# Other order of the first loads, counts in a shared PSUM bank, and an earlier weight fetch in a routing-attention and mixture-of-experts kernel

## The chip, the cores and the metric

The kernel runs on one core of one Trainium2 chip. The metric is the device time of one execution in microseconds (us); lower is better. TensorE (PE in the profile; PEld is its weight load) multiplies matrices, VectorE (DVE) and ScalarE (ACT) work elementwise, GpSimd (POOL) makes constants and here issues the indirect transfers, SyncE (SP) issues most of the other transfers. Each engine runs its own list of instructions in order and waits on semaphores for the others.

## The reference

Two stages. Attention, in which a query sees only the keys that fall into its own cluster, feeds a mixture of experts, in which each token goes to one expert.

```python
batch, n_heads, seq, head_dim = (4, 8, 768, 64);  n_clusters = 16
q_assign = argmax(einsum('bhsd,hcd->bhsc', q_n, c_n))        # q_n, k_n, c_n: rows over their norms
k_assign = argmax(einsum('bhsd,hcd->bhsc', k_n, c_n))
mask = q_assign[:, :, :, None] == k_assign[:, :, None, :]
scores = where(mask, q @ k^T / sqrt(64), -1e9)
x = softmax(scores) @ v                                      # then to [3072 tokens, 512]

N, D, E, F = (3072, 512, 8, 1024)
logits = x @ w_gate                                          # [3072, 8]
expert_idx = argmax(logits);  gate_w = softmax(logits)[expert_idx]
for e in range(E):                                           # tokens sorted by expert
    y[tokens of e] = relu(x[tokens of e] @ w1[e]) @ w2[e]
out = gate_w * y                                             # in the tokens' own order
```

Everything is float32. How many tokens an expert gets is known only on the chip.

## The kernel before

**Order.** Both parts are written under a manual schedule: the order of the program text is the order of each engine's list. The pools of tiles decide when a buffer may be written again. Of PSUM, pool `ps_s` holds three double banks `sps` for scores, and pool `ps_m` two banks `mps`, which attention outputs, sums, cluster scores and counts take in turn.

**Attention.** The 32 heads are taken as 16 pairs; pair `n` belongs to batch `n // 4`. A pair has 12 units, two halves of the queries by six blocks of keys. A unit is `score` (float32 products of `qT` and `kT` and, on top in the same bank, bfloat16 products of the cluster masks `mq` and `mk`, all at L370; then the exponential on ScalarE, L383, into `A`) and `add_up` (VectorE adds `A` into `acc`, L389). The products with `v` come after the units (`attend`, L395). Next to the units, `at_pair(n, u, f)` hangs other steps on unit `u` of pair `n`:

- `prepare(n + 1, step)` gets the next pair ready: its cluster scores (`similar`, L304), VectorE's choice of the nearest cluster (`assign0` to `assign2`, whose last result is `ohT`, L340), and the copies of it into `mk` on VectorE (L352) and `mq` on ScalarE (L350). Before it, `turn` (L272) transposes `q_in` and `k_in` to `qT` and `kT` on VectorE, two pairs ahead, between the halves of `attend`.
- `sum_up(n - 1)` at unit 2 makes the softmax sums and the gate's part on TensorE, in columns 0 to 191 of an `mps` bank; `weights_of(n - 1)` reads them on VectorE.
- Routing of a batch, in the pairs after it: `gate`, `gate_exp`, `gate_sum`, `choose`, then `count` (two 128 x 8 matmuls, L526 and L527, into an `mps` bank of their own) and `number` (VectorE, L532 to L539, which makes the places `pos_i`; `run` at L533 is the running count; then six indirect transfers from POOL, L541, into the list of tokens `tokens_of`). For batch 2 all of this is packed into pairs 12 and 13, since the first expert turns need it: `rank_first` (L576) picks their experts, `first_turns` (L782) reads their numbers into registers, fetches their token lists (`places`, from `tokens_of` into `sf`) and the weights of turn 0.

**Start.** `load(n)` issues the inputs of a pair. For pair 0, `q` and `k` go as one half on SP's queue and one half on ScalarE's, then `v_in` on SP's queue. `load(1)` follows at once. Then come the constants, TensorE's transposes of the pair 0 inputs and of the normed centroids `cn` (L262), `first_turn` (their copies out of PSUM), `cT` on VectorE, two ScalarE-queue stores of `cT` to memory (`c_normed`, L289), and nine small VectorE copies (L293 to L298) of constants that POOL has made. `prepare(0, ...)` runs through all its steps, and `routing_constants` (POOL) follows.

**Expert turns.** Ten turns `s`, each for one expert and a fixed number of its tokens: 288 and 288 for the two that start on the first three batches alone, then 256, 288, 288, 384, 416, 416, 448, 128. `layer1` (L881 on) forms the first product from seven half-size products per half of the features, in banks `bank` and `sbank`; it calls a hook after each, units 0 to 13 of `h1`. It wants four sums of the weights' quarters, `A[0]` to `A[3]` (`w1_sums`, L743, 1.23 us each on VectorE, `A[1]` from `A[2]`, `A[3]` from `A[1]`), and VectorE adds (L860) between its products. `layer2` (L985 on) does the same for full pairs of row tiles with `V[0]` to `V[3]` (`w2_sums`), with the hooks of `h2`; its results `z` go out through POOL's indirect transfers (L977). The hooks prepare the next turns: `places`, `indices`, `gather` (POOL's indirect loads of rows), `weigh` (VectorE, `xw`), `take` and `turn_rows` (the rows transposed, `xT`), `x_sums`, `first_weights` and `second_weights` (2 MB each, from SP's queue, into one of two sets of buffers, `wa` and `wb`, by turns), and the weights' sums at the units listed in `when`.

In turn 1, `weigh(2)` is at unit 6 of layer 1, `take(2)` and `first_weights(2)` at unit 7, `second_weights(2)` at unit 8, and the sums for turn 2 at units 2 to 6 of layer 2. In turn 0, `places(2)` is at unit 3 of layer 2.

Of the kernel before, what the change touches and what calls it, by code (L numbers as in the profile page):

```python
# [8 lines left out]
F32 = mybir.dt.float32  # L9
# [24 lines left out]
def kernel(  # L34
# [11 lines left out]
    nc = tc.nc  # L46
    B, H, S, D = q.shape
    C = centroids.shape[1]
    P = 128
# [63 lines left out]
    def iota(name, shape, pattern, base, mult):  # L113
        ti = consts.tile(shape, I32, name=name + "_i")
        tf = consts.tile(shape, F32, name=name)
        nc.gpsimd.iota(ti, pattern=pattern, base=base, channel_multiplier=mult)
        nc.gpsimd.tensor_copy(tf, ti)
        return tf
# [44 lines left out]
    with tc.manual_schedule(), ExitStack() as actx:  # L163
# [12 lines left out]
        def load(n):  # L176
            b, hp = divmod(n, HP)
            for d, src, name in ((QIN, q, "q_in"), (KIN, k, "k_in")):
                t = d[n] = ld.tile([P, NI, Q4], F32, name=name)
                if n == 0:  # L180
                    t = d[n] = t.rearrange("p i d -> p (i d)").rearrange("p (j a d) -> p j a d", a=2, d=D)
                    for a in range(2):
                        (nc.sync, nc.scalar)[a].dma_start(out=t[:, :, a, :], in_=src[0, a].rearrange("(p j) d -> p j d", j=NQ))
                    continue
                for r in range(4):
                    s = src[b, 2 * hp + r // 2, :, Q4 * (r % 2) : Q4 * (r % 2 + 1)]
                    nc.sync.dma_start(
                        out=t[Q4 * r : Q4 * (r + 1)].rearrange("t (j a) d -> t j a d", a=4),
                        in_=s.rearrange("(a t j) d -> t j a d", a=4, j=NQ),
                    )  # L190
            VIN[n] = ldv.tile([P, 2, NQ, D], F32, name="v_in")
            for a in range(2):
                nc.sync.dma_start(
                    out=VIN[n][:, a], in_=v[b, 2 * hp + a].rearrange("(p j) d -> p j d", j=NQ)
                )

        cin = consts.tile([P, D], F32)
        nc.scalar.dma_start(out=cin, in_=centroids.rearrange("h c d -> (h c) d"))
        for n in range(2):
            load(n)  # L200

        csq = consts.tile([P, D], F32)
        cs2 = consts.tile([P, 1], F32)
# [5 lines left out]
        nc.scalar.activation(warm, cnrm, AF.Exp, scale=0.0)  # L209
        MQ = [msk.tile([P, S], BF16, name=f"mq{i}") for i in range(2)]  # L210
        MK = [msk.tile([P, S], BF16, name=f"mk{i}") for i in range(2)]
        for i in range(2):
            for t in (MQ[i], MK[i]):
                (nc.gpsimd if i else nc.vector).memset(t, 0.0)

        cT = consts.tile([P, HP, 2, C], F32)
        nc.vector.memset(cT, 0.0)
# [2 lines left out]
        for a in range(2):  # L220
# [2 lines left out]
                in_=moe_w_gate.rearrange("(h a d) e -> a d h e", a=2, d=D)[a],  # L223
            )
        make_identity(nc, ident)
        first_c = iota("first_c", [P, C], [[-1, C]], C, 0)
        ones_s = consts.tile([P, 2, Q4], F32)
        nc.gpsimd.memset(ones_s, 0.0)
# [55 lines left out]
        cv = cps[:, 0:P].rearrange("p (h a c) -> p h a c", a=2, c=C)  # L284
        for a in range(2):
            nc.vector.tensor_copy(cT[D * a : D * (a + 1), :, a, :], cv[D * a : D * (a + 1), :, a, :])
        first_turn(1)
        for a in range(2):
            nc.scalar.dma_start(  # L289
                out=cn_d.rearrange("(h a) d c -> a d h c", a=2)[a], in_=cT[D * a : D * (a + 1), :, a, :]  # L290
            )
        first_cb = consts.tile([P, C], BF16)
        nc.vector.tensor_copy(first_cb, first_c)  # L293
        ksc2 = consts.tile([P, 2], F32)
        kscn2 = consts.tile([P, 2], F32)
        for r in range(4):
            nc.vector.tensor_copy(ksc2[Q4 * r : Q4 * (r + 1)], ksc)
            nc.vector.tensor_copy(kscn2[Q4 * r : Q4 * (r + 1)], kscn)  # L298

        def similar(n):  # L300
            ps = ps_m.tile([P, 512], F32, name="mps")
# [40 lines left out]
        def place(n, w):  # L342
            t, m = OH[n], (MQ, MK)[w][n % 2]
            for h in range(2):
                for a in range(2):
                    g = 2 * w + h
                    dst = m[D * a : D * a + Q4, HS * h : HS * (h + 1)]
                    src = t[Q4 * g : Q4 * (g + 1), :]
                    if w == 0:
                        nc.scalar.copy(dst, src)  # L350
                    else:
                        nc.vector.tensor_scalar(  # L352
                            dst, src, scalar1=ksc2[Q4 * g : Q4 * (g + 1), a : a + 1],
                            scalar2=kscn2[Q4 * g : Q4 * (g + 1), a : a + 1], op0=ALU.mult, op1=ALU.add,
                        )
            if w == 0:
                OH.pop(n)
# [44 lines left out]
                nc.scalar.copy(OT[n][:, h * HS : (h + 1) * HS], O.pop((n, h))[:, 0:HS])  # L402


        def sum_up(n):

            ps = SL[n] = ps_m.tile([P, 512], F32, name="mps")
            for w in range(3):
                for qd in range(4):
                    if w < 2:  # L410
                        c0 = TC * Q4 * (qd % 2)
                        lhsT, rhs = ones_s[:, w, :], ACC[n, qd // 2][:, w, c0 : c0 + TC * Q4]
                    else:
                        lhsT, rhs = wgt[:, n % HP, :], OT[n][:, TC * Q4 * qd : TC * Q4 * (qd + 1)]
                    nc.tensor.matmul(  # L415
                        ps[Q4 * qd : Q4 * (qd + 1), 0 : TC * Q4], lhsT=lhsT, rhs=rhs, start=(w == 0), stop=(w == 2),
                    )
# [103 lines left out]
            nc.vector.tensor_copy(last, pr[:, :, TC - 1])  # L521

        def count(b):
            last = LAST.pop(b)
            cps = CPS[b] = ps_m.tile([P, 512], F32, name="mps")
            nc.tensor.matmul(cps[:, 0:E], lhsT=lt_strict, rhs=last, start=True, stop=True)  # L526
            nc.tensor.matmul(cps[:, E : 2 * E], lhsT=ones_sq, rhs=last, start=True, stop=True)  # L527

# [232 lines left out]
        for n in range(NPAIR):  # L761
            if n:
                at_pair(n, 2, sum_up, n - 1)
                at_pair(n, 2, weights_of, n - 1)
                at_pair(n, 4, rows, n - 1)
                at_pair(n, 4, store, n - 1)
            for u, step in ((2 if n else 4, 1), (5, 2), (7, 3), (8, 4), (11, 5)):
                at_pair(n, u, prepare, n + 1, step)
        for b in range(B - 1):
            n = HP * (b + 1)  # L770
            last = b == B - 2
            at_pair(n, 5 if last else 10, gate, b)
            at_pair(n, 8 if last else 11, gate_exp, b)
            at_pair(n + (not last), 10 if last else 3, gate_sum, b)
            at_pair(n + (not last), 8 if last else 9, choose, b)
            at_pair(n + 2 - last, 0 if last else 4, count, b)
            at_pair(n + 2 - last, 1 if last else 6, number, b)
        n = HP * (B - 1)
        slots = range(len(EARLY))
        at_pair(n + 1, 3, rank_first)  # L780

        def first_turns():  # L782
            for s in slots:
# [44 lines left out]
    with tc.manual_schedule(), ExitStack() as ectx:  # L828
# [269 lines left out]
        for s in range(NS):  # L1098
# [5 lines left out]
            if s == 0:  # L1104
                at(h1, 2, sum_up, n - 1)
                at(h1, 2, weights_of, n - 1)
                at(h1, 3, gate, B - 1)
                at(h1, 3, gate_exp, B - 1)
                at(h1, 5, gate_sum, B - 1)
                at(h1, 5, choose, B - 1)  # L1110
                at(h1, 8, count, B - 1)
                at(h1, 9, number, B - 1)
                at(h1, 11, rows, n - 1)
                at(h1, 11, store, n - 1)
                at(h1, 12, rank_all)
                at(h2, 0, rank_rest)
                at(h2, 3, places, 2)
                at(h2, 7, indices, 2)
                at(h2, 7, gather, 2)
            if s == 3:  # L1120
# [2 lines left out]
            if s < last:  # L1123
                if 2 < s + 2 <= last:
                    places(s + 2)
                if s == 0:
                    first_weights(1)
                elif s > 1:
                    take(s + 1)
                if s == 1:  # L1130
                    at(h1, 6, weigh, 2)
                    at(h1, 7, take, 2)

                    at(h1, 7, first_weights, 2)
                    at(h1, 8, second_weights, 2)
                else:
                    second_weights(s + 1)
                if 0 < s <= last - 2:
                    at(h2, 0, first_weights, s + 2)

                if s == 0:
                    when = ((h2, 1), (h2, 2), (h2, 4), (h2, 5), (h2, 7), (h2, 7))
                elif s == 1:
                    when = ((h2, 2), (h2, 3), (h2, 4), (h2, 5), (h2, 6), (h2, 6))
                else:
                    when = ((h1, 9), (h1, 10), (h2, 1), (h2, 2), (h2, 2), (h2, 5))
                if GR[s + 1]["T"] >= 2 * P:
                    for (h, i), f, a in zip(when, (w1_sums,) * 4 + (w2_sums,) * 2, (2, 1, 0, 3, 2, 0)):
                        at(h, i, f, s + 1, (a,), nc.vector)
                at(h2, 1 if s == 1 else 3, turn_rows, s + 1)  # L1150
                if GR[s + 1]["T"] >= 2 * P:
                    at(h2, 1 if s == 1 else 4, x_sums, s + 1)
# [287 lines left out]
```

## Time and profile before

| what | value |
|---|---|
| runs | 682.28, 679.32, 677.63 us; median 679.32 us |
| the profiled execution | 680.02 us, of which the span of the trace is 678.2 us |
| mean granted TensorE clock | 0.989 of full |
| instructions in the trace | 11364 |
| read from and written to HBM | 74.10 MB and 20.70 MB |
| SP's queue q1 | 43.8% of the 16 DMA engines' time |
| attention pair, usual length by the start of its units | 19.74 us |
| same, pairs 6 and 10 (a batch's routing in them) | 21.02 us |
| same, pair 13 (batch 2's routing, packed) | 22.95 us |

The profile comes from one execution. Busy time is a share of the span. A wait is the idle time of an engine ahead of an instruction, put down to what released it. Rows of the timeline begin with the start of the first instruction and the length of the stretch, both in us, and name line, engine, operation and tiles (out<-in); a bracket gives the idle time ahead of it and its releaser. The slices of the page cut the span into 40 parts of 17.0 us; a digit is a share in tenths.

The three places that the change touches lie at the first 40 us (start), around 276 to 303 us (pairs 13 and 14), and at 363 to 405 us (the end of turn 0 and turn 1).

### The profile page before, as it was taken

What the parts mean: (1) busy time and instruction counts of PE and PEld (TensorE: products, weight loads), DVE (VectorE), ACT (ScalarE), POOL (GpSimd) and SP (SyncE); (2) the same over time, 40 slices, a digit from 0 to 9 for tenths busy, and PEclk for the clock granted to TensorE, in tenths of its full rate; (3) what the DMA queues carried; (4) which work ended last, traced back from release to release, by engine and by line L of the source; (5) the groups of instructions that cost most, each with busy time, mean ns of one, the idle gap of its engine ahead of it and who ended that gap; (6) DMA issues with size and microseconds to landing.
All of it is one profiled execution on the core that took longest, in us unless ns stands there. A gap on an engine that the chain in (4) does not pass through costs nothing.

```text
span 678.2 us, 11364 instructions
## 1 busy us (share of the span) xinstructions
PE 648.1 (96%) x4210; PEld 424.3 (63%) x4210; DVE 512.5 (76%) x909; ACT 301.0 (44%) x524; POOL 124.4 (18%) x145
## 2 busy tenths in 40 slices
PE   4999999999999999999999989999999999999993
PEld 2445444455444454444484879978797977869771
DVE  5889999999999999999887788886868375562300
ACT  2756556667556566556432323333231332413210
POOL 4000000012000300222113522324241422040010
PEclk9899999999999999999999989999999999999997
DMA  9723455433455434356473498667494837523010
GB/s 185 144 51 73 88 94 94 67 70 69 80 94 94 73 73 78 63 152 197 113 264 96 147 388 281 227 261 251 196 288 175 271 127 218 201 73 135 7 49 17
DMA packets 191807, 95.37 MB, mean 141 GB/s; under 512 B 155967, under 2 KB 173887, under 8 KB 190464
## 3 DMA queue, kind: packets, MB, share of 16 engines
q1 hardware_dynamic: 184016, 81.12, 43.8%
q0 software_dynamic: 4928, 12.97, 5.8%
q10 hardware_dynamic: 2800, 0.48, 0.4%
q8 instruction: 35, 0.57, 0.4%
q14 instruction: 28, 0.23, 0.1%
HBM read 74.10 MB, written 20.70 MB: 140 GB/s over the span
## 4 chain that ended last, share of the span: by engine, by line
PE 52%; issue 27%; DVE 8%; DMA 5%; POOL 5%; SPq 2%; ACT 1%; POOLq 0%; DVEq 0%; ACTq 0%
PE sps L370 19%; PE mps L395 15%; PE bank L902 4%; PE bank L1003 3%; PE sbank L902 3%; POOL out_dram L977 3%; PE sbank L1003 2%; PE mps L415 2%; PE bank L1022 2%; PE mps L304 2%; DVE acc L389 2%; POOL xg L672 1%; DMA w<-in_moe_w_dram 1%; DVE a L723 1%; DVE xw L689 1%
## 5 line engine op out<-in xcount | busy, mean ns | idle before, releaser
L383 ACT ACTIVATE A<-sps 128x768 f32<-128x768 f32 x192 | 153.1, 811 | 47.3 <-PE sps L370 46.2
L370 PE MATMUL sps<-qT,kT 64*128 64x384 f32 x768 | 160.2, 496 | 1.9 <-ACT A L383 1.9
L389 DVE TENSOR_TENSOR acc<-acc,A 128x768 f32<-128x768 f32 x128 | 121.4, 948 | 9.7 <-ACT A L383 3.3
L395 PE MATMUL mps<-A,v_in 128*64 128x384 f32 x768 | 127.4, 488 | 0.0
L370 PEld LDWEIGHTS sps<-qT,kT 64*128 64x128 f32 x768 | 66.8, 188 | 57.8 <-issue 51.0
L395 PEld LDWEIGHTS mps<-A,v_in 128*64 128x64 f32 x768 | 53.8, 137 | 70.5 <-issue 62.2
L977 POOL DMA_INDIRECT out_dram<-z,si x30 | 47.8, 1594 | 199.9 <-DVE z L860 170.7
L541 POOL DMA_INDIRECT tokens_of<-tg,pos_i x24 | 27.1, 1128 | 291.8 <-DVE pos_i L539 145.8
L370 PE MATMUL sps<-mq,mk 64*128 64x384 bf16 x384 | 63.4, 324 | 2.7 <-ACT mq L350 2.7
L1022 PE MATMUL bank<-w,h 128*128 128x512 f32 (+2 forms) x224 | 64.4, 596 | 0.0
L672 POOL DMA_INDIRECT xg<-x_rows,gi x30 | 41.4, 1382 | 50.7 <-DVE gi L662 19.3
L350 ACT COPY mq<-ohT 32x384 bf16<-32x384 bf16 x64 | 32.6, 510 | 38.7 <-DVE ohT L340 29.5
L902 PE MATMUL sbank<-xc,a 128*128 128x144 f32 (+4 forms) x288 | 48.0, 310 | 1.4 <-ACT h L920 0.7
L902 PE MATMUL bank<-xT,w 128*128 128x144 f32 (+4 forms) x288 | 47.8, 309 | 0.0
L902 PEld LDWEIGHTS bank<-xT,w 128*128 128x128 f32 x288 | 43.9, 191 | 2.6 <-issue 2.2
L1022 PEld LDWEIGHTS bank<-w,h 128*128 128x128 f32 (+2 forms) x224 | 24.6, 151 | 32.5 <-issue 32.3
L902 PEld LDWEIGHTS sbank<-xc,a 128*128 128x128 f32 x288 | 43.3, 190 | 2.1 <-issue 1.2
L860 DVE TENSOR_TENSOR h<-sbank,p 128x288 f32<-128x288 f32 (+4 forms) x18 | 9.2, 513 | 46.8 <-PE sbank L902 45.7
L370 PEld LDWEIGHTS <-mk 64*128 64x128 bf16 x384 | 19.5, 94 | 28.2 <-DVE mk L352 3.3
L920 ACT ACTIVATE h<-h 128x288 f32<-128x288 f32 (+4 forms) x36 | 17.6, 488 | 41.4 <-DVE h L860 32.6
L689 DVE TENSOR_TENSOR xw<-xg,sf 128x256 f32<-128x256 f32 (+2 forms) x60 | 32.8, 607 | 2.2 <-DMA xg<-x_rows,gi 1.7
L389 DVE TENSOR_TENSOR acc<-A 128x768 f32<-128x768 f32 x32 | 30.3, 947 | 5.1 <-ACT A L383 5.0
(205 smaller groups left out, 884.5 us busy)
## 6 DMA issues: line engine op xcount, KB each, us to landing
w<-in_moe_w_dram SPq DMA_DIRECT2D x20, 2048.0 KB
v_in<-in_v_dram SPq DMA_DIRECT2D x32, 192.0 KB
x_rows<-x SPq DMA_DIRECT2D x64, 96.0 KB
turn_rows<-xw SPq DMA_DIRECT2D x23, 256.0 KB
q_in<-in_q_dram SPq DMA_DIRECT2D x60, 96.0 KB
k_in<-in_k_dram SPq DMA_DIRECT2D x60, 96.0 KB
xs<-turn_rows SPq DMA_DIRECT2D x16, 144.0 KB
xs<-turn_rows SPq DMA_DIRECT2D x8, 208.0 KB
```

The source lines that it names most:

```text
L350: nc.scalar.copy(dst, src)
L370: nc.tensor.matmul(SP[n, h, j][:, a, 0:HS], lhsT=kt[rows, j * P : (j + 1) * P], rhs=qt[rows, h * HS : (h + 1) * HS], start=first, stop=not ...
L383: nc.scalar.activation(A[n, h, j], ps[:, :, 0:HS], AF.Exp, scale=D**-0.5)
L389: nc.vector.tensor_tensor(ACC[n, h], first, A[n, h, j], op=ALU.add)
L395: nc.tensor.matmul(O[n, h][D * a : D * (a + 1), 0:HS], lhsT=VIN[n][:, a, j, :], rhs=A[n, h, j][:, a, :], start=(j == 0), stop=(j == NQ - 1),)
L541: ins = nc.gpsimd.indirect_dma_start(out=t_d[:, :], out_offset=bass.IndirectOffsetOnAxis(ap=pos_i[:, i : i + 1], axis=0), in_=tg[:, b, i, ...
L672: nc.gpsimd.indirect_dma_start(out=xg[0:m], out_offset=None, in_=x_d[0:rows_in, :], in_offset=bass.IndirectOffsetOnAxis(ap=g["gi"][0:m, j ...
L689: nc.vector.tensor_tensor(xw[0:m, :, :, d2 * a : d2 * (a + 1)], xg[0:m].rearrange("p (r a d b) -> p a r b d", r=HP, a=2, b=DB)[:, a], g["s ...
L902: nc.tensor.matmul(ps[:, f * T2 : (f + 1) * T2], lhsT=w[:, k, (2 * j + f) * P : (2 * j + f + 1) * P], rhs=x[:, k, :], start=first and f + ...
L977: ins = nc.gpsimd.indirect_dma_start(out=out[:, :], out_offset=bass.IndirectOffsetOnAxis(ap=GR[s]["si"][0:rows, j : j + 1], axis=0), in_=z ...
L1003: nc.tensor.matmul(ps[:, 0:H], lhsT=x[:, k, :], rhs=y[:, k, :], start=first and k == 0, stop=k == 3, skip_group_check=not first,)
L1022: nc.tensor.matmul(ps[i * m : (i + 1) * m, :], lhsT=h[:, f, j * P : j * P + m], rhs=w[:, f, :], start=(k == 0), stop=(k == FB // n - 1),)
```

## The change

It has three parts.

**Start.** `load(0)` no longer brings `v_in`; that moves into a function `load_v`. The two stores of `c_normed` go from ScalarE's queue to SP's, directly after `cT`; `load_v(0)` and all of `load(1)` are issued behind them. `MQ[1]` and `MK[1]` are zeroed on POOL after `ident`, not ahead of it. The nine small copies go from VectorE to POOL. Of pair 0's four `mq` copies, the two of the second half go from ScalarE to POOL.

**Counts.** For pairs other than the last, `sum_up` leaves its bank in `BANK`, and `count`, now always at unit 2 and registered after `sum_up` and the next pair's `similar`, writes into columns 256 on of that bank, where it took a bank of its own before. `weights_of` is registered after it. For batch 2, `choose` goes from unit 8 to 10 of pair 12, `gate_sum` from 10 to 9, `count` from unit 0 to 2 of pair 13, `number` from 1 to 3, `rank_first` from 3 to 4. For batches 0 and 1, `count` goes from unit 4 to 2 of pairs 6 and 10; `number` stays at unit 6.

**Turn 2's weights.** `first_weights(2)` goes from unit 7 of turn 1's layer 1 to unit 3 of turn 0's layer 2, behind `places(2)`. In turn 1, the sums `A[2]` and `A[1]` for turn 2 go from units 2 and 3 of layer 2 to units 9 and 10 of layer 1, and `A[0]` and `A[3]` from units 4 and 5 of layer 2 to units 2 and 3.

```diff
@@ load @@
+            if n:
+                load_v(n)
+
+        def load_v(n):
+            b, hp = divmod(n, HP)
             VIN[n] = ldv.tile([P, 2, NQ, D], F32, name="v_in")
@@
-        for n in range(2):
-            load(n)
+        load(0)
@@
-        for i in range(2):
-            for t in (MQ[i], MK[i]):
-                (nc.gpsimd if i else nc.vector).memset(t, 0.0)
+        for t in (MQ[0], MK[0]):
+            nc.vector.memset(t, 0.0)
@@
         make_identity(nc, ident)
+        for t in (MQ[1], MK[1]):
+            nc.gpsimd.memset(t, 0.0)
@@ after cT @@
+        for a in range(2):
+            nc.sync.dma_start(
+                out=cn_d.rearrange("(h a) d c -> a d h c", a=2)[a], in_=cT[D * a : D * (a + 1), :, a, :]
+            )
+
+        load_v(0)
+        load(1)
         first_turn(1)
-        for a in range(2):
-            nc.scalar.dma_start(
-                out=cn_d.rearrange("(h a) d c -> a d h c", a=2)[a], in_=cT[D * a : D * (a + 1), :, a, :]
-            )
         first_cb = consts.tile([P, C], BF16)
-        nc.vector.tensor_copy(first_cb, first_c)
+        nc.gpsimd.tensor_copy(first_cb, first_c)
@@
-            nc.vector.tensor_copy(ksc2[Q4 * r : Q4 * (r + 1)], ksc)
-            nc.vector.tensor_copy(kscn2[Q4 * r : Q4 * (r + 1)], kscn)
+            nc.gpsimd.tensor_copy(ksc2[Q4 * r : Q4 * (r + 1)], ksc)
+            nc.gpsimd.tensor_copy(kscn2[Q4 * r : Q4 * (r + 1)], kscn)
@@ place @@
-                        nc.scalar.copy(dst, src)
+                        (nc.gpsimd.tensor_copy if n == 0 and h else nc.scalar.copy)(dst, src)
@@ sum_up @@
             ps = SL[n] = ps_m.tile([P, 512], F32, name="mps")
+            BANK[:] = [ps] if n < NPAIR - 1 else []
@@ count @@
-            cps = CPS[b] = ps_m.tile([P, 512], F32, name="mps")
+            cps = CPS[b] = BANK.pop()[:, 2 * P : 4 * P] if BANK else ps_m.tile([P, 512], F32, name="mps")
@@ steps of the pairs @@
                 at_pair(n, 2, sum_up, n - 1)
-                at_pair(n, 2, weights_of, n - 1)
@@
-            at_pair(n + (not last), 10 if last else 3, gate_sum, b)
-            at_pair(n + (not last), 8 if last else 9, choose, b)
-            at_pair(n + 2 - last, 0 if last else 4, count, b)
-            at_pair(n + 2 - last, 1 if last else 6, number, b)
+            at_pair(n + (not last), 9 if last else 3, gate_sum, b)
+            at_pair(n + (not last), 10 if last else 9, choose, b)
+            at_pair(n + 2 - last, 2, count, b)
+            at_pair(n + 2 - last, 3 if last else 6, number, b)
+        for n in range(1, NPAIR):
+            at_pair(n, 2, weights_of, n - 1)
@@
-        at_pair(n + 1, 3, rank_first)
+        at_pair(n + 1, 4, rank_first)
@@ turn 0 @@
                 at(h2, 3, places, 2)
+                at(h2, 3, first_weights, 2)
@@ turn 1 @@
                     at(h1, 7, take, 2)
-
-                    at(h1, 7, first_weights, 2)
                     at(h1, 8, second_weights, 2)
@@
-                    when = ((h2, 2), (h2, 3), (h2, 4), (h2, 5), (h2, 6), (h2, 6))
+                    when = ((h1, 9), (h1, 10), (h2, 2), (h2, 3), (h2, 6), (h2, 6))
```

More of the change, by code (lines that the diff above doesn't have):

```diff
@@ L286 @@
             nc.vector.tensor_copy(cT[D * a : D * (a + 1), :, a, :], cv[D * a : D * (a + 1), :, a, :])
-        first_turn(1)
         for a in range(2):
-            nc.scalar.dma_start(
+            nc.sync.dma_start(
                 out=cn_d.rearrange("(h a) d c -> a d h c", a=2)[a], in_=cT[D * a : D * (a + 1), :, a, :]
             )
+        load_v(0)
+        load(1)
+        first_turn(1)
         first_cb = consts.tile([P, C], BF16)
-        nc.vector.tensor_copy(first_cb, first_c)
+        nc.gpsimd.tensor_copy(first_cb, first_c)
         ksc2 = consts.tile([P, 2], F32)
@@ L402, in attend @@
                 nc.scalar.copy(OT[n][:, h * HS : (h + 1) * HS], O.pop((n, h))[:, 0:HS])
+        BANK = []
         def sum_up(n):
             ps = SL[n] = ps_m.tile([P, 512], F32, name="mps")
+            BANK[:] = [ps] if n < NPAIR - 1 else []
             for w in range(3):
```

## The prediction

> **What bounds the kernel now.** I read the page first (shares, slices), then TensorE's waits, then the timelines of TensorE, VectorE and the queues where those waits lie.
>
> ```profile
> PE 648.1 (96%) x4210; PEld 424.3 (63%) x4210; DVE 512.5 (76%) x909; ACT 301.0 (44%) x524; POOL 124.4 (18%) x145
> PEclk9899999999999999999999989999999999999997
> ```
>
> TensorE is busy for 648.1 of 678.2 us: some 30 us of gaps and what a half clock stretches are all that reordering can win. TensorE's waits (us, times, longest) say where they are:
>
> ```profile
> PE sps L262 <- POOL kscn L241: 5.1, 1, 5.1
> PE sps L370 <- ACT mq L350: 2.7, 2, 2.5
> PE sbank L1003 <- DVE z L860: 2.6, 3, 2.0
> PE sps L262 <- DMA k_in<-in_k_dram: 1.6, 1, 1.6
> PE mps L304 <- DVE run L533: 1.5, 1, 1.5
> ```
>
> The change has a part at the last four. The 5.1 us ahead of the first transpose is put down to POOL, but `ident` was written by 3.62; the first `q` halves are what lands at 5.06, and they stay first. The start, from the timeline (start, length):
>
> ```profile
> 8.42 1.51 PE L262 MATMUL sps<-ident,k_in 128*128 128x128 f32 x6 [1.60 <-DMA k_in<-in_k_dram]
> 16.04 2.10 ACT L350 COPY mq<-ohT 32x384 bf16<-32x384 bf16 x4 [5.58 <-DMA tokens_of<-none]
> 18.16 2.21 ACT L383 ACTIVATE A<-sps 128x768 f32<-128x768 f32 x3
> ```
>
> The `k` transposes wait for their load, a VectorE chain follows to `ohT` (16.00), then ScalarE makes four copies before its first exponential. The second place is pair 13 to 14. VectorE's waits from 241 to 331 us are this one row, and its gap ends at 240.74; with it, both engines where pair 15's clusters are scored:
>
> ```profile
> DVE acc L389 <- ACT A L383: 0.8, 1, 0.8
> 301.90 0.93 DVE L272 STREAM_TRANSPOSE kT<-k_in 128x768 f32<-128x768 f32 x1
> 302.82 0.49 PE L304 MATMUL mps<-qT,cT 128*32 128x384 f32 x2
> 302.89 0.52 PE L304 MATMUL mps<-kT,cT 128*32 128x384 f32 x2
> ```
>
> For 90 us VectorE waits for nothing, and at 302.83 it hands over `kT` just as TensorE asks (302.89). There the two engines are level. The third place is turn 1, VectorE's and TensorE's rows:
>
> ```profile
> 383.54 1.23 DVE L723 TENSOR_TENSOR v<-w,v 128x1024 f32<-128x1024 f32 x1
> 384.67 0.46 DVE L860 TENSOR_TENSOR h<-sbank,p 128x288 f32<-128x288 f32 x1
> 385.19 1.25 PE L902 MATMUL sbank<-xT,a 128*128 128x144 f32 x8
> 398.00 1.23 DVE L723 TENSOR_TENSOR a<-w 128x1024 f32<-128x1024 f32 x1 [1.77 <-DMA w<-in_moe_w_dram]
> 399.26 1.23 DVE L723 TENSOR_TENSOR a<-w,a 128x1024 f32<-128x1024 f32 x1
> 400.40 0.42 DVE L860 TENSOR_TENSOR z<-sbank,p 128x256 f32<-128x256 f32 x1
> 400.87 3.66 PE L1003 MATMUL sbank<-w,hs 128*128 128x256 f32 x8 [2.02 <-DVE z L860]
> 404.36 1.05 PE L902 MATMUL bank<-xT,w 128*128 128x128 f32 x8
> ```
>
> Turn 2's weights land at 398, two sums queue ahead of the add that TensorE waits for, and the eight matmuls after the gap take 3.49 us to the next row where the block before took 1.73 (395.23 to 396.96). The stretches' table (PE busy, PEld busy, DVE, ACT, POOL, granted clock) says why:
>
> ```profile
> 397.50:400.80 3.30, 1.35 (x7) 0.84 (x5) 2.77 (x4) 0.00 (x0) 0.00 (x0) 1.00 1.05 408
> 400.90:404.20 3.30, 3.30 (x8) 2.67 (x9) 3.28 (x4) 0.00 (x0) 1.64 (x1) 0.50 1.09 454
> ```
>
> So the place costs 2.02 + 1.76 = 3.78 us.
>
> **Part A, the start.** Before, `v_in(0)` and pair 1's loads are issued from 2.25 on and share the DMA engines with the second half of `k` (ScalarE's queue, issued 1.92). The other half had landed by 6.27, when ScalarE's queue, which waits for it, issues `wgt`. Without the company both should be there by then, and TensorE, busy with `q` and `cn` until 6.82, goes on at 6.85 instead of 8.42: -1.57. `ohT` moves from 16.00 to 14.43. ScalarE then makes two `mq` copies (0.51 each), POOL the other two, needed only half a pair later. The first exponential waits for the second masked matmul, 17.13 - 1.57 = 15.56, plus 0.32 and 0.06: 15.95 instead of 18.16, that is -2.21. The nine small VectorE copies cost nothing before (VectorE then waited 0.58 for TensorE) and nothing on POOL: nine of 0.18 after 5.0 end at 6.7, and `first_cb` is wanted at 12.3.
>
> What is moved must still fit. SP's queue: `c_normed` waits for `cT` (7.35), two issues of 0.69 to 8.8, `v_in(0)` 1.12 to 9.9, `q_in(1)` 2.71 to 12.6, `k_in(1)` 2.88 to 15.5; from the end of four `xs` issues to their use it is 2.8 us (363.86 to 366.61), so `k_in(1)` is there at 18.3. VectorE wants it at 17.0, stalls 1.3 and ends `kT(1)` at 19.3; TensorE asks at about 20. Hidden, narrowly; VectorE has waits of 0.41, 0.83 and 1.73 (23.24, 25.02, 39.64) to catch up. `tokens_of<-none` and pair 2's loads behind them slip 3 us and are wanted after 34. POOL's 4.6 us of routing constants (4.95 to 9.6) move behind its `mq` copies, to 16 to 21, beside VectorE's dense work. The Trainium skill, "GPSIMD Engine Reference", Key points, says that GpSimd shares its SBUF interfaces with VectorE and contends with its two-input operations, and Engine selection gives elementwise work to VectorE. The trace has no such overlap to price; nearest are POOL's one-input copies (0.22 for 24 columns). By the rule VectorE could lose up to those 4.6 us; its 3 us of waits take most, so I book 0, and 1.6 at the bad end. A half clock lies at 18.6 to 21.9 in this execution; it would come again, over a thinner stretch: -0.4 (0 to -0.8). A: -2.6 (-1.0 to -3.5).
>
> **Part B, the counts.** In pairs 6 and 10 the two count matmuls (0.26 each) only move two units earlier: 0. The attention output's first bank now waits for `number`'s read: L533 ends at 228.47 + 0.17 = 228.64, TensorE starts there at 228.89; hidden by 0.25, else a few tenths. In pair 13 the bank's wait (1.50) goes. What is late next: `kT(14)` (281.13, a wait of about 0.5) stays. Pair 13 takes 22.95 us (276.25 to 299.20), pair 6 with the same work 21.02, so TensorE gains 1.93. But VectorE does the same operations in another order and gains nothing: at 302.89 TensorE must again wait for `kT(15)`. Kept: 0.1. `number` now stands behind two adds and `weights_of`, so pos_i comes at 286.0 instead of 283.1; `tokens_of` lands some 3 us later (about 296.4), SP's `sf` issues end at 299 and land by 301, VectorE reads at 302.76: hidden. `rank_first` is 1.8 us later; SP's register loads follow its stores anyway. B: -0.1 (-1.9 to +0.4).
>
> **Part C, turn 2's weights.** The 2 MB go out behind `places(2)`, about 367; the DMA slices there are nearly idle until 378, so at the 5 to 9 us that such a fetch takes (389.04 to 398) they are in before 376. SP's `sf(3)` stands behind them and is wanted at 377.81: hidden. The wait at 398 goes, and w2(2) comes earlier. But the first-layer sums `A[2]` and `A[1]` now stand at layer-1 units 9 and 10 of turn 1, in VectorE's list right behind `v` (383.54) and ahead of the add of 384.67, whose bank the matmuls of 385.19 overwrite. VectorE is late there (its `xw` waits 0.58 and 1.12 for gathers), so 2.40 us (398.00 to 400.40) go straight in: the add ends at 387.53, TensorE stalls 2.4. Layer 2 follows 2.4 later on both; `A[0]` and `A[3]` still stand ahead of the `z` add: 398.63 + 2.40 = 401.03 against a wanted 398.70 + 2.40, a further 0.4. Then the clock. The Trainium skill, "TensorE: Matmul & The Clock Gate", Why this matters, has it fall after a whole window of idling, about 3.4 us, so a gap of 2.4 would be free: cost 2.8, gain 1.0. The row above speaks against it: 2.02 us of gap were enough. By the row 1.7 comes on top, less the 0.4 it hides: cost 4.1, loss 0.3. I take the row three times in four: C about 0 (+1.2 to -3.8, the last if VectorE isn't late).
>
> **Sum.** -2.6 - 0.1 + 0 = -2.7 against the profiled execution's 680.02 (span 678.2, 1.8 around it): 677.3. The median of the runs is 679.32, 0.7 lower, so 676.6.
>
> **The rivals.** (1) VectorE isn't the bound: its rows are close-packed only because TensorE feeds them so. Then B keeps 1.9 and C 2.8: 676.6 - 1.8 - 2.8 = 672.0. For it: up to pair 12 VectorE waits 0.5 to 0.8 for ScalarE in most second pairs (202.41, 240.74). Against: none from 241 to 331. (2) The start doesn't carry: `k_in(1)` or POOL holds VectorE beyond its slack, A is 0 to -0.6: 679.0. (3) Slower: the 2 MB collide. If SP reaches the fetch only after about 373 (its `places` wait for tokens), the gathers of turn 2's rows at 374.87 and 378.10 queue beside 2 MB, `xw` slips by up to 5 us, and with it the add of 384.67: 5 more of stall and no gain in turn 1, 676.6 + 5.5 = 682.1. It decides from 2.8 us of slip on. Against: SP issued those loads at 365.34 unhurried. That the fetch isn't earlier at all is excluded by SP's list.
>
> **How the numbers follow.** My forecast 0.62 (own range 674.6 to 678.6), rival 1 0.17, rival 2 0.13, rival 3 0.08. Leaving out a tenth at each end: 672.0 to 680.0. One per cent, 6.8 us, is about what a measurement of this kernel can tell from no change: faster means below 672.5, which is over half of rival 1 and an edge of mine, 0.13; slower, above 686.1, only rival 3 doubled, 0.02.
>
> **What would show it.** `k` transposes at 6.9 and the first exponential near 16; no wait on `run` in pair 13 and in its place waits for `kT` in pairs 13 and 14; `a` sums before the add in turn 1's layer 1, and TensorE waiting there for over 2 us, with no wait for weights after. It is wrong if TensorE waits less than 1 us there, or if pair 14's end moves by more than the start.

## The result, and the profile after

| | before | changed |
|---|---|---|
| median | 679.55 us (22 runs) | 677.25 us (22 runs) |
| ratio | | 0.9966, 95% interval 0.9953 to 0.9979 |
| profiled execution | 680.02 us, span 678.2 | 678.35 us, span 676.3 |
| mean granted clock in it | 0.989 | 0.989 |

The change takes 2.3 us off (1.4 to 3.2 by the interval), which is clear of noise but less than the one per cent that the prediction calls faster. All lines of the code after the edits are numbered 5 to 14 higher.

TensorE's waits of the changed kernel (us, times, longest):

```profile
PE sbank L916 <- DVE h L874: 3.5, 3, 2.5
PE sps L379 <- DVE mk L361: 2.9, 2, 2.7
PE mps L427 <- DVE acc L398: 0.9, 2, 0.7
PE sbank L1017 <- DVE z L874: 0.6, 2, 0.4
```

Beside the list of before: the waits for `k_in` (1.6), for `run` (1.5) and the 2.0 of the `z` add are gone. New are 2.5 at an `h` add and 0.7 at `acc`. So two of the three waits removed have a new one close by; the wait for `k_in` has none. The three places, from the timelines (start, length), first the start:

```profile
6.85 1.51 PE L267 MATMUL sps<-ident,k_in 128*128 128x128 f32 x6
14.29 1.04 ACT L359 COPY mq<-ohT 32x384 bf16<-32x384 bf16 x2 [5.41 <-DVE ohT L348]
15.90 2.22 ACT L392 ACTIVATE A<-sps 128x768 f32<-128x768 f32 x3 [0.57 <-PE sps L379]
14.36 2.03 DVE L361 TENSOR_SCALAR mk<-ohT,ksc,kscn 32x384 bf16<-32x384 bf16 x4
18.23 0.98 DVE L277 STREAM_TRANSPOSE kT<-k_in 128x768 f32<-128x768 f32 x1 [0.82 <-DMA k_in<-in_k_dram]
```

The `k` transposes follow the `q` ones with no gap, and the first exponential is at 15.90, 2.26 earlier. The four `mk` copies take 2.03, where before they took 1.59:

```profile
16.04 1.59 DVE L352 TENSOR_SCALAR mk<-ohT,ksc,kscn 32x384 bf16<-32x384 bf16 x4
```

`k_in(1)` holds VectorE for 0.82. Then pairs 13 and 14; the first row is of the kernel before, the others of the changed kernel:

```profile
299.20 0.92 PE L370 MATMUL sps<-qT,kT 64*128 64x384 f32 x4
295.15 0.92 PE L379 MATMUL sps<-qT,kT 64*128 64x384 f32 x4
298.88 0.97 DVE L277 STREAM_TRANSPOSE qT<-q_in 128x768 f32<-128x768 f32 x1
299.78 0.94 DVE L277 STREAM_TRANSPOSE kT<-k_in 128x768 f32<-128x768 f32 x1
299.02 0.68 PE L427 MATMUL mps<-acc,ones_s 128*32 128x192 f32 x10 [0.73 <-DVE acc L398]
```

`kT(15)` starts 2.12 earlier (299.78 after 301.90): the start's gain, nothing more. TensorE was further ahead (pair 14 starts at 295.15, before at 299.20, so 4.05 earlier), and gives the difference back, here by waiting for `acc` ahead of its sums. Last, turn 1, with the stretches' table (PE busy, PEld busy, DVE, ACT, POOL, granted clock) below:

```profile
383.24 1.20 DVE L736 TENSOR_TENSOR v<-w,v 128x1024 f32<-128x1024 f32 x1
384.37 1.21 DVE L736 TENSOR_TENSOR a<-w 128x1024 f32<-128x1024 f32 x1
385.69 1.23 DVE L736 TENSOR_TENSOR a<-w,a 128x1024 f32<-128x1024 f32 x1
386.83 0.45 DVE L874 TENSOR_TENSOR h<-sbank,p 128x288 f32<-128x288 f32 x1
387.33 1.25 PE L916 MATMUL sbank<-xT,a 128*128 128x144 f32 x8 [2.54 <-DVE h L874]
388.42 3.49 PE L1017 MATMUL bank<-w,h 128*128 128x256 f32 x8
404.50 1.05 PE L916 MATMUL bank<-xT,w 128*128 128x128 f32 x8
```

```profile
385.13:388.55 3.42, 1.22 (x9) 1.22 (x10) 2.50 (x4) 0.73 (x2) 1.20 (x1) 1.00 0.68 198
388.55:391.96 3.41, 3.41 (x13) 2.20 (x15) 2.55 (x4) 0.76 (x3) 0.00 (x0) 0.50 0.84 231
```

The two sums (`a`) stand ahead of the `h` add; TensorE waits 2.54 and then runs eight matmuls in 3.49 us at half a clock. Before, the same eight took 1.89:

```profile
386.27 1.89 PE L1003 MATMUL bank<-w,h 128*128 128x256 f32 x8
```

Turn 2's first matmul is at 404.50, before at 404.36. So in this one execution turn 2 starts no earlier at all, although the start gained 2.2 us: the gain of the span shows only later (turn 5 starts at 486.47 after 488.41). The experiments sort out where each part's gain goes.

### The profile page after: what moved, and what is told of

The parts are those of the page before. It is cut to its first block, busy times and chain, and to the rows that moved or that the text cites. A ratio compares the mean times of both kernels' runs of the same rounds, so it can differ in the third digit from the quotient of the medians.

```text
span 676.3 us, 11363 instructions
## 1 busy us (share of the span) xinstructions
PE 649.1 (96%) x4210; PEld 424.6 (63%) x4210; DVE 511.9 (76%) x900; ACT 300.4 (44%) x522; POOL 126.7 (19%) x156
## 4 chain that ended last, share of the span: by engine, by line
PE 58%; issue 26%; DVE 7%; POOL 5%; DMA 2%; ACT 0%; POOLq 0%; SPq 0%; DVEq 0%; ACTq 0%
PE sps L379 20%; PE mps L404 15%; PE bank L1017 5%; PE bank L916 4%; PE sbank L916 4%; PE sbank L1017 3%; POOL out_dram L991 3%; PE mps L427 2%; PE mps L312 2%; PE bank L1036 2%; DVE acc L398 1%; POOL xg L685 1%; DMA xg<-x_rows,gi 1%; POOL tokens_of L554 1%; DVE a L736 1%
```

## The experiments

Each is compared with runs of the kernel before on the same chip; ratios are to those, and a difference in us is the ratio's distance from 1 times 680.

**The parts alone.** Three kernels, each the kernel before with one part of the diff: the start, the counts, the weights with their sums.

> Part A alone (the start). Carried theory: the first exponential near 16.0 us and every pair's matmuls 2.2 earlier than before; VectorE is the only pacer behind it, so kT(15) is also 2.2 earlier and the whole gain reaches the end: 2.2 us less than the kernel before. Lost theory (what the traces of before and after hint at): the lead is there to pair 15, but turn 0's xs transfers land less than 1 us earlier, TensorE's lead at the first matmul of turn 1's second product is under 0.5, and the time falls by 0 to 1 us only.

> Part B alone (the counts). Theory that VectorE is the bound from 241 to 331 us: no wait on run in pair 13, pair 14 begins some 1.9 earlier, but kT(15) ends within 0.2 of 302.83 and TensorE waits there or at pair 13's sums; time within 0.5 of before. Rival (TensorE's wait is what counts): kT(15) moves with it, turn 0 begins 1.9 us earlier, time 1.9 less. Third possibility: tokens_of, 0.8 later by the traces, moves nothing.

> Part C alone (turn 2's weights and the two sums in layer 1). Swap theory: TensorE waits about 2.5 us at 387 for the add behind the two sums, eight matmuls after it at half clock cost 1.7 more, no wait at 400; the turn after starts within 0.5 of before; time within 0.5 of before. Rival that the part gains: the stall at 387 is under 1 us and the time falls by 3.

| kernel | ratio, 95% interval | us |
|---|---|---|
| start alone | 0.9987, 0.9977 to 0.9997 | -0.9 |
| counts alone | 1.0005, 0.9991 to 1.0020 | +0.3 |
| weights and sums alone | 0.9987, 0.9972 to 1.0003 | -0.9 |

Counts alone, TensorE's waits from 270 to 331 us and VectorE's row:

```profile
PE mps L418 <- DVE acc L389: 0.7, 1, 0.7
302.14 0.94 DVE L272 STREAM_TRANSPOSE kT<-k_in 128x768 f32<-128x768 f32 x1
```

The wait on `run` is gone, TensorE waits 0.7 for `acc` at pair 14's sums instead, and `kT(15)` starts at 302.14, 0.24 later than before, with the same first exponential (18.18). The rival, 1.9 us to gain, is out. Weights alone, TensorE in turn 1 and the window around it:

```profile
386.77 1.25 PE L902 MATMUL sbank<-xT,a 128*128 128x144 f32 x8 [2.60 <-DVE h L860]
387.85 1.89 PE L1003 MATMUL bank<-w,h 128*128 128x256 f32 x8
```

```profile
382.52:385.94 3.42, 1.65 (x14) 1.43 (x12) 3.32 (x4) 0.14 (x1) 2.94 (x2) 1.00 0.72 227
385.94:389.35 3.41, 2.58 (x15) 2.42 (x16) 1.81 (x4) 1.47 (x4) 0.00 (x0) 1.00 0.70 197
```

The stall is the same (2.60), but here no half clock follows: the matmuls behind it take 1.89. The start alone brings 0.9 us, less than half of the 2.2 at the first exponential. Two runs bear on that: the kernel before once more, and the kernel before with nothing of part A but the order of the loads (the memsets, the small copies and all `mq` copies as before):

```diff
-        for n in range(2):
-            load(n)
+        load(0)
...
+        for a in range(2):
+            nc.sync.dma_start(
+                out=cn_d.rearrange("(h a) d c -> a d h c", a=2)[a], in_=cT[D * a : D * (a + 1), :, a, :]
+            )
+
+        load_v(0)
+        load(1)
         first_turn(1)
```

> The kernel before, unchanged, for a second profile: how far one execution's stages vary. From the end of kT(15) to turn 0's xT the first profile has 28.4 us, the five others of this study 29.05 to 29.8. If the first was a lucky draw, this one has 29 or more and turn 0's second product waits for its sums here too; if 28.4 returns, the new start has cost something there. Half clocks: each should follow a window of 3.41 us in which TensorE was under 0.45 busy, as in the six traces so far (0.28 to 0.44 with a half clock after, 0.48 and above without).

> Only the order of the loads of part A (v and pair 1 behind cT, c_normed on SP), all mq copies on ScalarE, small copies on VectorE as before. By the prediction's steps: k transposes at 6.9 to 7.1, first exponential 18.16 - 1.57 = 16.6. VectorE's four mk copies take 1.6 us again, not 2.0, if it was POOL's two copies beside them that stretched them in the changed kernel (2.03); if they take 2.0 here too, POOL isn't the cause.

A single execution each, so without an interval: 680.44 us for the kernel before, 679.12 us for the loads only. Timelines of the loads only:

```profile
14.18 1.60 DVE L359 TENSOR_SCALAR mk<-ohT,ksc,kscn 32x384 bf16<-32x384 bf16 x4
14.17 2.10 ACT L357 COPY mq<-ohT 32x384 bf16<-32x384 bf16 x4 [5.26 <-DVE ohT L347]
16.30 2.21 ACT L390 ACTIVATE A<-sps 128x768 f32<-128x768 f32 x3
```

With all `mq` copies on ScalarE the `mk` copies take 1.60 again, so the 0.43 us more in the changed kernel come from POOL's work beside them. POOL's two copies there:

```profile
14.31 1.05 POOL L359 COPY mq<-ohT 32x384 bf16<-32x384 bf16 x2 [7.89 <-DVE ohT L348]
```

One by one, the four `mk` copies take 0.56 and 0.52 us beside these two, then 0.38 and 0.47 beside POOL's memsets; in the loads only and before each takes 0.37 or 0.38. So the two copies account for 0.33 of the 0.43. In return ScalarE is free sooner. From the start of the `mq` copies to the first exponential it is 2.13 us in the loads only and 2.12 or 2.13 in all five profiles with the old start, but 1.61 or 1.62 (once 1.78) in the eight of this study with the whole new start. So POOL's share of the `mq` copies brings 0.5 us. That the loads only are at 16.30, close to the mean of the eight (16.21, from 15.84 to 16.57), is because `ohT` came early in this one execution.

The second profile of before has 29.2 us from the end of `kT(15)` to turn 0's `xT` (302.73 to 331.91); the first has 28.4, the changed kernel 29.65. The first was the shortest draw, so most of the lead that the changed kernel seems to lose in turn 0 is the jitter of a transfer (before `xT`, VectorE waits 1.51 and 2.31 us for `xs` in the two profiles of before). The other sign named in the expectation, a wait of turn 0's second product for its sums, did not come.

**The half clock.** In these traces the granted clock changes only in steps of 3.413 us, called windows here; where they lie against the program differs from run to run. TensorE's busy time in windows with gaps, and the clock granted in the next one, from the stretches' tables:

| kernel, window from | PE busy, us | next window |
|---|---|---|
| early second-layer weights (below), 12.11 | 0.50 | 0.50 |
| early second-layer weights (below), 411.46 | 0.61 | 0.50 |
| before, 15.15 | 0.96 | 0.50 |
| loads only, 12.96 | 0.96 | 0.50 |
| changed, 13.08 | 0.99 | 0.50 |
| changed, 385.13 | 1.22 | 0.50 |
| before, 397.45 | 1.40 | 0.50 |
| before (second profile), 398.01 | 1.48 | 1.00 |
| changed (second profile), 14.52 | 1.50 | 0.50 |
| loads only, 398.69 | 1.53 | 0.50 |
| weights and sums alone, 382.52 | 1.65 | 1.00 |
| fetch only (below), 13.78 | 1.67 | 1.00 |
| changed (second profile), 383.16 | 1.87 | 1.00 |

Up to 1.40 us of 3.41 the next window was at half clock every time, from 1.65 on never; at 1.48, 1.50 and 1.53 it went both ways. So the border of 0.45 in the expectation, 1.54 us, is not sharp. A gap of 2.0 to 2.6 us crosses it or doesn't by where a window's edge cuts it. The loads only have two half windows in a row:

```profile
16.38:19.79 3.41, 2.63 (x10) 1.47 (x12) 1.47 (x3) 2.75 (x4) 0.00 (x0) 0.50 0.96 274
19.79:23.20 3.41, 3.41 (x16) 0.86 (x14) 3.10 (x4) 1.00 (x2) 0.00 (x0) 0.50 0.87 253
```

What does a half window cost? From the start of the first exponential to the end of `kT(15)` it is 283.2 us in both profiles with the old start and no half clock in it. It is 284.7 and 284.9 in the two with one (the counts-alone run, whose work differs, left aside), 284.5 to 284.9 in the seven with the new start and the same work up to there, which all have one, and 286.1 in the loads only with its two. So one half window costs about 1.6 us, two cost about 2.9, and nothing else behind the first exponential does: `k_in(1)` holds VectorE for 0.82 to 1.91 us in the new start, and the stretch is no longer for it.

In the start, all eight profiles with the whole new start have a half clock, but only three of the five with the old start. `kT(15)` ends at 302.84 and 302.73 in the old start with a half clock, at 300.86 and 301.68 in the two without, and at 300.97 on average in the seven with the new start. So the new start is 1.8 us ahead of an old one with half clock, but only 1.1 ahead of the average old one. The time gives 0.9 (0.2 to 1.6), which fits. That the new start brings the half clock more often is not shown: eight of eight against three of five can be chance, the share was not varied by itself, and the mean granted clock of all runs differs little (0.9907 in 22 runs of the start alone, 0.9914 in the 44 of before beside them; by estimate from 3.41 us in 677, one half window is 0.0025).

**VectorE as the bound.** In the changed kernel, `rank_first` is done twice:

```diff
         at_pair(n + 1, 4, rank_first)
+        at_pair(n + 1, 4, rank_first)
```

> The changed kernel with the thirteen small VectorE operations of rank_first done twice in pair 13: 2.2 us more VectorE work, the results the same. If VectorE is the bound there: kT(15) ends 2.2 later, TensorE's wait at pair 14's sums grows from 0.7 to 2.5 to 2.9, and as much as the later stages pass on shows at the end: 1 to 2.2 us more than the changed kernel (677.3), so 678.3 to 679.5. If VectorE has slack in pairs 13 to 15: nothing moves at the end, within 0.5.

Measured: 1.0002 (0.9989 to 1.0015) against the changed kernel's 0.9966, that is 2.4 us more. The timeline of VectorE and TensorE's wait from 250 to 310 us:

```profile
302.53 0.94 DVE L277 STREAM_TRANSPOSE kT<-k_in 128x768 f32<-128x768 f32 x1
```

```profile
PE mps L427 <- DVE acc L398: 1.5, 1, 1.5
```

`kT(15)` is 2.75 later, of which 0.6 was there already at 21 us (TensorE's `similar` for pair 1). So 2.2 us more of VectorE work in pair 13 come out as 2.15 at `kT(15)`, and, within the intervals, in full at the end. TensorE's wait at the sums grew by 0.8 only, not by 1.8 or more as expected; another 0.4 is a new wait for `mk` just before.

**Where the two sums stand.** The changed kernel with the old places of the sums, and the kernel before with the early fetch only:

```diff
-                    when = ((h1, 9), (h1, 10), (h2, 2), (h2, 3), (h2, 6), (h2, 6))
+                    when = ((h2, 2), (h2, 3), (h2, 4), (h2, 5), (h2, 6), (h2, 6))
```

> The changed kernel, but the sums for turn 2 stay where they were before, at units 2 to 5 of turn 1's layer 2, with the early fetch. If the two sums in layer 1 are what eats part C's gain: no stall at 387, no wait of VectorE for w at 398, the z add near 398.6, TensorE waits there under 0.3 us and the clock stays full; 3.4 to 3.8 us less than the changed kernel, near 673.6. If instead the stall at 387 comes from late gathers (xw) and not from the sums: it stays, over 1 us, and the time is within 1 of the changed kernel. If the gain is lost again at a later anchor (turn 2's xs or weights of turn 3): the lead at the first matmul of turn 2 is 3.4 and shrinks below 1.5 by turn 4.

> The changed kernel once more, beside the next ones on one chip: 2.3 us below the kernel before, as first measured. Of the two gaps that could bring a half clock (start, and TensorE's 2.5 us at 387), each does so or not with where the 3.41 us windows happen to lie: a window under about 0.45 busy is followed by half a clock, one above is not; in this profile the same rule.

> The changed kernel with turn 2's sums in layer 2, as in the run before, for a direct comparison. If the two early sums cost what the stall at 387 shows (2.5 us, and a half clock in most runs): 2 to 3.5 us less than the changed kernel. If turns 2 and 3 take the lead back (VectorE waiting for sf and weights there, as its first profile shows): 0 to 1 us less.

> The kernel before with the early fetch alone: start, counts and the places of the sums as before. Against part C alone (0.9 less than before, with the two sums in layer 1): no stall at 387, no wait for w at 398. If the sums' place costs, 2 to 3 us less than before; if turns 2 and 3 level it, about 1 less, the same as part C alone.

| kernel | ratio, 95% interval | `kT(15)` ends | turn 2 starts | turn 5 starts |
|---|---|---|---|---|
| before, first profile | | 302.84 | 404.36 | 488.41 |
| before, second | | 302.73 | 404.15 | 488.50 |
| weights and sums alone | 0.9987, 0.9972 to 1.0003 | 300.86 | 402.30 | 485.64 |
| changed, first | 0.9966, 0.9953 to 0.9979 | 300.72 | 404.50 | 486.47 |
| changed, second | 0.9947, 0.9924 to 0.9969 | 301.45 | 403.11 | 485.32 |
| late sums, first | 0.9959, 0.9943 to 0.9975 | 301.37 | 400.19 | 486.10 |
| late sums, second | 0.9950, 0.9928 to 0.9972 | 300.47 | 399.39 | 484.58 |
| before with early fetch, late sums | 0.9964, 0.9950 to 0.9978 | 301.68 | 400.88 | 485.74 |

From turn 5 on all these profiles are alike (189.8 to 190.3 us to the end of the span), so the table holds what differs. Read it by stages. From `kT(15)` to turn 2 it is 101.4 and 101.5 us before. With the early fetch and the early sums it is 101.4 to 103.8: no gain there, and a loss in the profile whose stall brought a half clock. With the late sums, where the stall at 387 and the wait for weights are both gone, it is 98.8 to 99.2, a gain of 2.2 to 2.7. From turn 2 to turn 5 the order turns round: 84.05 and 84.35 before, 82.0 to 83.3 with the early sums, 84.9 to 85.9 with the late ones. So beside the changed kernel the late sums are 4.3 and 3.7 us ahead at turn 2 (first profiles, then second), but only 0.4 and 0.7 at turn 5, and the time is the same.

Without the other two parts the late sums are 1.6 us better than the early ones (0.9964 against 0.9987, and the intervals overlap); whether the sums' place is worth 0 or 1.5 us in the end stays open. One thing is plain: the early fetch alone, with nothing else of the change, takes off 2.4 us (1.5 to 3.4), as much as the whole change. VectorE's waits from 395 to 480 us and TensorE's from 330 to 480 in the late sums, second profile:

```profile
DVE gi L675 <- DMA sf<-tokens_of: 2.7, 3, 1.5
DVE v L736 <- DMA w<-in_moe_w_dram: 1.5, 1, 1.5
PE sbank L916 <- DVE h L874: 2.4, 4, 1.0
PE sbank L916 <- ACT sbank L940: 1.0, 1, 1.0
```

In turns 2 and 3 VectorE stands at `gi` until the token list has landed, with the next adds behind it, and TensorE waits for some of those (0.49 us at 412.90 and 0.97 at 436.00). With the later turn 2 of the changed kernel VectorE's waits at `gi` are 0.3 and 0.7 in its two profiles, against 3.1 and 2.7 here. Two attempts at them. First, turn 3's second-layer weights ahead in SP's queue, on top of the late sums (the edit of `when` as above):

```diff
-                else:
+                elif s != 2:
                     second_weights(s + 1)
...
+                if s == 1:
+                    at(h2, 6, second_weights, 3)
                 at(h2, 6 if s == 1 else 4, weigh, s + 2)
```

> The changed kernel with the late sums, and turn 3's second-layer weights fetched at unit 6 of turn 1's layer 2, ahead of turn 3's row stores in SP's queue, not behind turn 3's xs in turn 2. If that load is what takes the lead of turn 2 back (VectorE waits 2.0 us at 422.8 for it): the wait goes, TensorE's lead at turn 3 stays 1.5 us longer, and the time is 1 to 1.5 below that of the late sums alone (677.6), near 676.3. If the lead is lost to sf (VectorE waits 1.3 at 434) and to VectorE itself: within 0.5 of the late sums. If the earlier 2 MB delay xs or sf: slower.

Slower: 1.0028 (1.0013 to 1.0044), 4.7 us over the late sums. Its timelines (SP's issue, VectorE, TensorE):

```profile
399.26 0.38 SPq L105 DMA_DIRECT2D w<-in_moe_w_dram  x1
406.30 0.39 SPq L659 DMA_DIRECT2D sf<-tokens_of  x1
411.36 0.16 DVE L675 SCALAR_TENSOR_TENSOR gi<-sf 128x2 int32<-128x2 f32 x1 [4.39 <-DMA sf<-tokens_of]
415.73 2.08 PE L916 MATMUL sbank<-xT,a 128*128 128x128 f32 x8 [3.66 <-DVE h L874]
```

The small list, issued 7 us behind the 2 MB, takes 5.06 us from issue to its first reader (in the late sums' first profile 1.7, from 407.45 to 409.16); TensorE waits 3.66 and two half windows follow. Second, the reading of the lists later, on top of the late sums and in every turn from 2 on:

```diff
-                at(h1, 5 if s == 2 else 4, indices, s + 2)
-                at(h1, 5 if s == 2 else 4, gather, s + 2)
+                at(h1, 4 if s == 1 else 7, indices, s + 2)
+                at(h1, 4 if s == 1 else 7, gather, s + 2)
```

> As the late sums, and from turn 2 on the reading of the token lists (indices) and the gathers stand at unit 7 of layer 1, not at 5 or 4, so that VectorE no longer stands waiting for sf with the next adds behind it (1.06, 0.30, 1.32 us in turns 2 and 3). If that wait is what took the lead back: no wait of VectorE for sf, TensorE's waits for h in turns 2 and 3 gone, time 1 to 2 us below the late sums. If the weights' arrival (v, 2.0 us at 422.8) or later gathers set the pace: within 0.5, and VectorE's wait moves to v or to xw.

0.9921 (0.9891 to 0.9952) at 675.70 us, the best of all: 5.4 us below before, and 1.7 below the median of the late sums that ran beside it, though those two intervals overlap. VectorE's waits in the same stretch have no row for `gi` any more; of its waits for transfers this one remains, with TensorE's below it:

```profile
DVE v L736 <- DMA w<-in_moe_w_dram: 1.5, 1, 1.5
PE sbank L916 <- DVE h L874: 1.9, 3, 1.0
```

TensorE's wait at `sbank` for ScalarE is gone, and one of the four at `h`; three stay, though the expectation had them gone. Turn 2 starts at 400.12 and turn 5 at 483.09: 4.2 and 5.3 us ahead of before. In this profile, with the wait at `gi` out of VectorE's way, the lead of turn 2 reaches turn 5. The gathers moved in the same edit, so that the wait alone is the cause is likely but not shown.

## Why the prediction was right, and where not

- **The whole.** 676.6 was named, 677.25 measured; -2.7 expected, -2.3 found (in the second set of runs -3.6, from -2.1 to -5.2). The division over the parts was wrong, so that the total came out close is partly luck: A brought 1.7 us less than booked, B 0.4 less, C 0.9 more. The parts found alone (-0.9, +0.3, -0.9) sum to -1.5, just inside the interval of the whole.
- **Part A up to the first exponential** held: transposes 6.85 (6.85 named), exponential 15.90 (15.95), VectorE's stall for `k_in(1)` 0.82 to 1.91, mean 1.29, in eight profiles (1.3). Between averages the exponential gains 1.9 us, not 2.2 (16.21 in eight profiles, 18.07 in the five with the old start). The term that was mis-sized is the half clock, entered as -0.4 with bounds of 0 and -0.8. One costs about 1.6 us in the new start as in the old one, so the thinner stretch spared nothing; and since two of the four old profiles with the same work had none, the new start lost 0.7 us on average at `kT(15)` (1.8 less 1.1). A came to -0.9 in place of -2.6, just outside its own range and nearly the second rival's size, but not by `k_in(1)` or POOL.
- **POOL beside VectorE**: 0 was booked, with the Trainium skill's rule ("GPSIMD Engine Reference", Key points) held against it at up to 4.6 us. The runs show 0.43 us on the `mk` copies. These have one tensor as input, so the two-input operations that the prediction speaks of are hardly tested: beside POOL's constants stood only one, the `acc` add at 19.13 (0.92 us, before 0.96). POOL's `mq` copies were to bring 0.64 and bring 0.5.
- **Part B** held to 0.4 us: VectorE does the same work in another order, and TensorE's 1.9 turns into another wait. It was expected at `kT`; it came one step earlier in VectorE's list, at `acc`. The 0.5 us at `kT(14)` that were to stay did not come. One reading was off: `run` (L533) in pair 10 starts at 228.55, not 228.47, so the slack there was 0.17 us. The first rival is excluded here by the counts alone and, for pair 13, by the doubled `rank_first`.
- **Part C** held in turn 1: a stall of 2.4 was named, 2.54 came; the half clock behind it came in two of four profiles with the early sums (three in four was taken; the other is the doubled rank's), and turn 2's start moved by 0.14. The reason that the rule of a whole idle window ("TensorE: Matmul & The Clock Gate", Why this matters) was set aside stands: windows 15 to 41% busy were followed by half a clock every time. Two things were mis-sized. The old place was priced at 3.78 us with its half clock, but that came in two of the five profiles with the late fetch; without stall and wait the stretch to turn 2 gains 2.2 to 2.7. And what comes after turn 2 was put at nothing: with the early sums the 0.9 us are won only there, in turns 2 to 4, by TensorE waiting less (0.6 us from turn 2 to turn 5 in the changed kernel, about 2 before). Why these turns run closer was not varied. The first rival's C of 2.8 is near what the early fetch brings alone with the late sums (2.4).
- **The third rival**, 2 MB in the way of small transfers, did not occur at its place (VectorE's waits for `xg` were 0.48 and 1.25, before 0.58 and 1.12). Something like it is what made the early second-layer weights slower.

## What to carry to other kernels

A wait removed is worth what is left after the next engine in the chain has had its say: put each part's gain against the other engine's own timeline, not only at the next instruction but some stages on, and ask there which wait grows when this one shrinks. An engine that is the bound should not stand in its list at a small transfer's landing while adds for another engine are queued behind it; here moving the read later went with a gain of some 1.7 us, and sending a large transfer ahead of it cost 4.7. When a change has several parts, run each one alone: here one moved line gave as much as all of it. And with gaps near the border of a clock window, one profile is one draw: two of the same kernel belong side by side before a difference of 2 us is put down to the edit.

## What was unexpected of the hardware

- A window of 3.413 us does not have to be idle to bring half a clock: 0.50 to 1.40 us of TensorE work in it (15 to 41%) brought it each time, 1.65 (48%) and more never, and from 1.48 to 1.53 it went both ways. A window at half clock can be followed by another: those of 2.56 (early second-layer weights) and 2.63 us busy (loads only) were, those of 2.90 and more were not.
- A small load behind 2 MB in one queue landed after 5.06 us, where it took 1.7 us otherwise, though the big one had been issued 7 us before it. The DMA engines were 0.86 busy meanwhile, 0.13 in the late sums' second profile.
- Two POOL copies of 32x384 bfloat16 stretched the two VectorE operations of the same shape beside them from 0.37 to 0.56 and 0.52 us, though these read one tensor each.
